# Chunked attention and a multiplicative feed-forward: other transfer costs and first loads in the planner, zero matmuls in early gaps, a last tile in smaller parts

## The chip, the core and the metric

The kernel runs on one core of a Trainium2 chip. The metric is device time in microseconds (us) of one execution; several executions give a median. A profile of a separate execution gives the span from the first to the last instruction and what each engine did. The engines are TensorE (PE in the views, its weight loads PEld), VectorE (DVE), ScalarE (ACT), GpSimd (POOL) and SyncE (SP). Transfers run on the core's 16 DMA engines. GpSimd issues the loads that cast from f32 to bf16, SP issues the outputs and the transposing transfers.

## The reference

```python
# q, k, v: (8 batches, 8 heads, 576 positions, 64), float32; chunks of 64 positions
scores = scale * np.matmul(q_c, k_c.transpose(0, 1, 2, 4, 3))
scores = scores - np.max(scores, axis=-1, keepdims=True)
attn = np.exp(scores)
attn = attn / (np.sum(attn, axis=-1, keepdims=True) + 1e-09)
out = np.matmul(attn, v_c)
...
x = np.ascontiguousarray(attn_out.transpose(0, 2, 1, 3)).reshape(B * S, H * D)
...
a = x @ w1          # x: 4608 x 512, w1 and w2: 512 x 1024
b = x @ w2
h = a * b @ w3      # w3: 1024 x 1024
return (h @ w_out).astype(np.float32)   # w_out: 1024 x 512
```

## The kernel before

The 4608 tokens are cut into 36 groups of 128 (two chunks of 64 positions of all eight heads). Nine tiles of four groups each (512 tokens) go through the feed-forward. The kernel uses that (a*b) @ w3 @ w_out is (a*b) @ (w3 @ w_out), and first makes the 1024 x 512 product w3o.

A group passes these steps (function `add_group`). Loads of q and k into the tile `raw` (L261, from GpSimd). They are transposed, either by eight TensorE matmuls with the identity (L311, with copies to kT and qd), or, from group 12 on, by a transposing transfer from SP (L315, kqT<-raw, called turning here), with two copies to qd. Scores are eight matmuls of 64 columns (L339, p_sc). VectorE takes the maximum (L347) and subtracts it (L351), ScalarE takes the exponential (L355), VectorE sums (L359) and scales (L365, result `an`). `an` is transposed by four TensorE matmuls and a copy (L370), or, from group 24 on, by a transfer from SP (L321, at<-an). Values are eight matmuls of 64 columns (L381, p_av), and a copy writes the group's columns of xt. The buffers for `raw` are six, so the load of q and k for a group waits for an earlier group's transposition.

The product w3o takes eight steps (`add_w3o`): eight transposes of one block of w3 (L422), a copy, eight matmuls of 512 columns (L433, in two parts, one for each load of w_out), a copy. It runs in between the first groups.

A tile (`add_tile`) makes for each of eight column blocks j the products with w1 and w2 (L463, four matmuls of 512 columns each), a copy of the one (ScalarE) and the multiplication (VectorE, L472, abT). For each of its four groups follow eight matmuls with w3o (L488), a copy to o_sb and an output from SP (L497). The last group of the last tile has its 512 output columns in two halves.

The order of everything is set by a planner in the kernel (`Plan.run`) that plays the work through with costs given in microseconds: for each engine it picks, of the operations that are ready at that moment, the one with the lowest key (its due time), then the instructions are written in the order so found. Each engine then works strictly in that order, so an operation that waits longer on the chip than in the plan holds up all behind it on its engine. Loads keep the order of the list LOADS, and then go by groups with the v of a batch ahead of its first use. The planner shares the transfer engines between the queue of GpSimd and that of SP, lets each have eight transfers under way, and takes a transfer as usable a `lag` after its end. `LATE` shifts the keys of a group.

Of the kernel before, what the change touches and what calls it, by code (L numbers as in the profile page):

```python
# [14 lines left out]

LOADS = [('qk', 2), ('w3', 3, 4), ('qk', 0), ('qk', 3), ('ident',), ('qk', 1), ('w3', 5, 6), ('w3', 2, 3),
         ('wo', 0, 4), ('wo', 4, 8), ('w3', 0, 1), ('w3', 6, 7), ('v', 0), ('qk', 4), ('w3', 7, 8), ('qk', 5), ('w12', 0,
         2), ('w12', 6, 8), ('w12', 4, 6), ('qk', 6), ('qk', 7), ('w3', 1, 2), ('w12', 2, 4), ('w3', 4, 5), ('qk', 8),  # L20
         ('v', 1), ('qk', 9), ('qk', 10)]
TILES = [4] * 9

TURN_QK = [g >= 12 for g in range(36)]
TURN_A = [g >= 24 for g in range(36)]
LATE = 5


class Op:
# [124 lines left out]
def kernel(  # L154
# [48 lines left out]
    def ps(tag, shape, dt=f32):  # L203
        return psum.tile(shape, dt, tag=tag, name=tag, bufs=BUFS[tag])
# [39 lines left out]
    def load(cost, issue, emit, **kw):  # L244
        return plan.add("POOL", cost, 0, emit, lag=landing, issue=issue, **kw)
# [6 lines left out]
    def load_qk(g):  # L252
        (b0, c0), (b1, c1) = chunks(g)
        parts = [(slice(0, P), b0, c0, 2)] if b0 == b1 else [(halves[0], b0, c0, 1), (halves[1], b1, c1, 1)]
        box = raws[g] = {"ops": []}
        for w, src in enumerate((q, k)):
            for r, b, c, n in parts:
                def emit(eng, w=w, src=src, r=r, b=b, c=c, n=n):
                    if "t" not in box:
                        box["t"] = sb("raw", [P, 2, H, D])  # L260
                    nc.gpsimd.dma_start(box["t"][r, w], src[b, :, c * C:(c + n) * C, :].rearrange("h p d -> p h d"))  # L261
                box["ops"].append(load(0.43 * n, 0.5 + 0.2 * n, emit, takes=() if box["ops"] else ("raw",)))

    def load_v(b):
        v_got[b] = []
        for t in range(2):
            def emit(eng, t=t):
                nc.gpsimd.dma_start(vds[b % len(vds)][halves[t], :, :, t * D:(t + 1) * D].rearrange("p m c d -> p (m c) d"),  # L268
                                    v[b, NM * t:NM * (t + 1)].rearrange("h (c p) d -> p (h c) d", p=C))
            v_got[b].append(load(2.0, 1.17, emit, takes=() if t else ("vd",), after=(zero_v[b % len(vds)],)))  # L270

    def load_w12(j0, j1):
        for dst, w in ((w1_sb, moe_w1), (w2_sb, moe_w2)):
            for t in range(2):
                def emit(eng, dst=dst, w=w, t=t):
                    nc.gpsimd.dma_start(
                        dst[halves[t], :, j0 * P:j1 * P],
                        w[t * NM * D:(t + 1) * NM * D, j0 * P:j1 * P].rearrange("(m d) n -> d m n", d=D))
                o = load(0.33 * (j1 - j0), 0.62, emit)
        for j in range(j0, j1):  # L280
            w12_got[j] = o

    def load_w3(k0, k1):
        def emit(eng):
            nc.gpsimd.dma_start(w3_sb[:, k0:k1, :], moe_w3.rearrange("(ko p) n -> p ko n", p=P)[:, k0:k1, :])
        o = load(1.3 * (k1 - k0), 0.75, emit)
        for i in range(k0, k1):
            w3_got[i] = o

    def load_wo(k0, k1):  # L290
        def emit(eng):
            nc.gpsimd.dma_start(wo_sb[:, k0:k1, :], moe_w_out.rearrange("(ko p) n -> p ko n", p=P)[:, k0:k1, :])
        wo_got.append(load(0.64 * (k1 - k0), 0.75, emit))
        wo_cut.append((k0, k1))


# [2 lines left out]
    def add_group(g, kt, ks, ka, kv):  # L299
# [1 line left out]
        bc = chunks(g)  # L301
        qd = qds[g % len(qds)]

        turned = TURN_QK[g]

        def t_emit(eng):
            t = box["tr"] = ps("ffn", [P, 2, NM, P], bf)
# [78 lines left out]

        got = raws[g]["ops"]
        if turned:
            tr = kc = plan.add("SP", 1.75, kt, qk_turn, after=got, takes=("kqT",), uses=[(got[0], "raw")], lag=2.5, issue=1.3)
            held, cost = [(tr, "kqT")], (0.35, 0.6)  # L390
        else:
            tr = plan.add("PE", 0.46, kt, t_emit, after=got + [made_ident], takes=("ffn",), uses=[(got[0], "raw")], lag=0.2)
            held, cost = [(tr, "ffn")], (0.43, 0.66)
            kc = plan.add(("DVE", "ACT"), cost, kt, k_copy, after=(tr,), takes=("kT",), uses=held)
# [6 lines left out]
        ex = plan.add("ACT", 0.71, ks, exp_emit, after=[sd] + one_e, takes=("e",), uses=[(sd, "sd")])  # L401
        sm = plan.add("DVE", 0.95, ks, sum_emit, after=(ex,), lag=0.05)
        an = plan.add("DVE", 0.7, ks, norm_emit, after=(sm,), takes=("an",), uses=[(ex, "e")])
        if TURN_A[g]:
            ac = plan.add("SP", 0.88, ka, at_turn, after=(an,), takes=("at",), uses=[(an, "an")], lag=2.5, issue=1.3)
        else:
            at = plan.add("PE", 0.23, ka, at_emit, after=(an,), takes=("ffn",), uses=[(an, "an")], lag=0.2)
            ac = plan.add(("DVE", "ACT"), (0.43, 0.66), ka, at_copy, after=(at,), takes=("at",), uses=[(at, "ffn")])
# [42 lines left out]
    def add_tile(g0, n, kab, ko_):  # L451
        box = {}
        w = n * P
        x = xt[:, :, g0 * P:g0 * P + w]
        muls = []
        for j in range(FO):
            def mm(name, wt, j=j):
                def emit(eng):
                    if j == 0 and name == "a":
                        box["abT"] = sb("abT", [P, FO, TT])  # L460
                    t = box[name, j] = ps("ffn", [P, TT])
                    for ki in range(KO):
                        nc.tensor.matmul(t[:, :w], wt[:, ki, j * P:(j + 1) * P], x[:, ki, :],  # L463
                                         start=(ki == 0), stop=(ki == KO - 1))
                return emit

            def a_copy(eng, j=j):
                box["as", j] = sb("a_sb", [P, TT], f32)
                copy(eng, box["as", j][:, :w], box["a", j][:, :w])

            def mul(eng, j=j):
                nc.vector.tensor_mul(box["abT"][:, j, :w], box["as", j][:, :w], box["b", j][:, :w])  # L472

            dep = [w12_got[j]] + [x_done[g0 + i] for i in range(n)] + ([first] if j else [])
            a = plan.add("PE", 0.216 * n, kab(j), mm("a", w1_sb), after=dep, lag=0.2,
                         takes=("ffn", "abT") if j == 0 else ("ffn",))
            first = a if j == 0 else first
            b = plan.add("PE", 0.216 * n, kab(j) + 0.1, mm("b", w2_sb), after=dep, lag=0.2, takes=("ffn",))
            c = plan.add("ACT", 0.18 + 0.11 * n, kab(j) - 1, a_copy, after=(a,), takes=("a_sb",), uses=[(a, "ffn")])
            muls.append(plan.add("DVE", 0.18 + 0.13 * n, kab(j) - 1, mul, after=(b, c), uses=[(b, "ffn"), (c, "a_sb")]))  # L480
        last = g0 + n == NG
        cols = [(tk, 0, D_MODEL) for tk in range(n - last)]
        cols += [(n - 1, x, x + D_MODEL // 2) for x in (0, D_MODEL // 2)] if last else []
        for tk, x0, x1 in cols:
            def o_mm(eng, tk=tk, x0=x0, x1=x1):
                t = box["o", tk, x0] = ps("ffn", [P, D_MODEL])
                for ki in range(FO):
                    nc.tensor.matmul(t[:, :x1 - x0], box["abT"][:, ki, tk * P:(tk + 1) * P], w3o_sb[:, ki, x0:x1],  # L488
                                     start=(ki == 0), stop=(ki == FO - 1))

            def o_copy(eng, tk=tk, x0=x0, x1=x1):
                box["os", tk, x0] = sb("o_sb", [P, D_MODEL], f32)
                copy(eng, box["os", tk, x0][:, :x1 - x0], box["o", tk, x0][:, :x1 - x0])

            def o_out(eng, tk=tk, x0=x0, x1=x1):
                r0 = (g0 + tk) * P
                nc.sync.dma_start(out[r0:r0 + P, x0:x1], box["os", tk, x0][:, :x1 - x0])  # L497

            f = (x1 - x0) / D_MODEL
            key = ko_(tk) + 0.1 * (x0 > 0)  # L500
            o = plan.add("PE", 1.73 * f, key, o_mm, after=muls + w3o_done, takes=("ffn",), uses=[(first, "abT")], lag=0.2)
            c = plan.add(("ACT", "DVE"), (0.16 + 0.45 * f, 0.17 + 0.53 * f), key - 1, o_copy, after=(o,),
                         takes=("o_sb",), uses=[(o, "ffn")])
            outs.append((c, o_out))


# [59 lines left out]
```

## Time and profile before

| | us |
|---|---|
| median of 3 runs | 261.84 (258.81 to 266.3) |
| the profiled execution's own time | 264.01 |
| its span, first to last instruction | 262.2 |
| TensorE busy in it | 238.1 |
| VectorE busy | 175.0 |
| ScalarE busy | 145.9 |
| GpSimd busy (it issues loads) | 102.1 |

The span leaves out what lies around the first and the last instruction, 1.8 us of the profiled execution. In the rows of the views stand a start or a total in us, a length, the engine, the line of the kernel, and result<-operands by the program's names; x is a count. A wait names the engine and line that waited and what ended the wait. The row of slices cuts the span into 40 equal parts and gives the busy share of each in tenths. Matmuls overlap in the pipeline, so TensorE's price for one is read from the distance between starts, as the chain of waits has it, and not from its own duration.

### The profile page before, as it was taken

How to read it: one execution, taken by the hardware profiler on the slowest of the kernel's cores; microseconds unless marked ns; L12 is line 12 of the kernel's file. 1: busy time of each engine (PE TensorE's matmuls, PEld its weight loads, DVE VectorE, ACT ScalarE, POOL GpSimd, SP SyncE). 2: the span in 40 equal slices, each digit the busy share in tenths (PEclk: the TensorE clock that was granted, in tenths of full speed). 3: DMA queues.
4: the chain of work that ended last, by engine and by line, in shares of the span. 5: the costliest groups of instructions: out<-in, count | busy, mean ns of one | idle time of the engine just before them, and what ended most of it. 6: DMA issues, size and time to landing. Idle time of an engine off the chain costs nothing.

```text
span 262.2 us, 4687 instructions
## 1 busy us (share of the span) xinstructions
PE 238.1 (91%) x1736; PEld 125.8 (48%) x1768; DVE 175.0 (67%) x319; ACT 145.9 (56%) x248; POOL 102.1 (39%) x128
## 2 busy tenths in 40 slices
PE   0479999987999999999899999997979999999994
PEld 0354665545555555555445544453434544444442
DVE  5076888776989976997398977995958762223310
ACT  8262664765866684687367367564456554343332
POOL 8964689767785165228344712460000000000000
PEclk9999999999999999999999999999999999999998
DMA  6999999999999999999999999999996521112123
GB/s 54 163 201 172 169 183 168 175 147 114 156 186 136 153 199 135 176 180 187 149 198 157 166 121 182 197 132 153 194 152 160 103 80 42 41 40 80 42 79 121
DMA packets 155910, 37.01 MB, mean 141 GB/s; under 512 B 145008, under 2 KB 150384, under 8 KB 155888
## 3 DMA queue, kind: packets, MB, share of 16 engines
q0 software_dynamic: 118688, 19.41, 105.4%
q1 hardware_dynamic: 37200, 17.31, 38.0%
q8 instruction: 14, 0.23, 0.4%
q14 instruction: 8, 0.07, 0.1%
HBM read 38.80 MB, written 9.44 MB: 184 GB/s over the span
## 4 chain that ended last, share of the span: by engine, by line
PE 65%; DMA 17%; DVE 8%; issue 3%; ACT 2%; POOL 2%; ACTq 0%; DVEq 0%; POOLq 0%
PE ffn L463 34%; PE ffn L488 18%; DMA at<-an 7%; PE ffn L433 5%; DMA vd<-in_v_dram 4%; DMA kqT<-raw 3%; PE p_av L381 3%; DMA raw<-in_k_dram 3%; PE p_sc L339 2%; PE ffn L370 2%; DVE abT L472 2%; PE ffn L311 2%; DVE nm L347 1%; POOL raw L261 1%; DVE sd L351 1%
## 5 line engine op out<-in xcount | busy, mean ns | idle before, releaser
L463 PE MATMUL ffn<-xt,w_sb 128*128 128x512 bf16 x556 | 133.1, 379 | 2.0 <-DVE abT L472 1.1
L463 PEld LDWEIGHTS <-w_sb 128*128 128x128 bf16 x576 | 53.9, 98 | 59.8 <-issue 1.4
L472 DVE TENSOR_TENSOR abT<-a_sb,ffn 128x512 bf16<-128x512 f32 x72 | 49.0, 681 | 42.1 <-PE ffn L463 35.8
L488 PE MATMUL ffn<-w3o_sb,abT 128*128 128x512 bf16 (+1 forms) x287 | 66.4, 373 | 0.5
L223 ACT COPY a_sb<-ffn 128x512 f32<-128x512 f32 x72 | 41.9, 583 | 27.3 <-PE ffn L463 27.0
L261 POOL DMA_DIRECT2D raw<-in_q_dram x40 | 34.2, 857 | 37.9 <-DMA vd<-in_v_dram 14.4
L261 POOL DMA_DIRECT2D raw<-in_k_dram x40 | 34.1, 854 | 31.0 <-DMA vd<-in_v_dram 21.8
L488 PEld LDWEIGHTS <-abT 128*128 128x128 bf16 x296 | 28.0, 98 | 29.5
L223 ACT COPY o_sb<-ffn 128x512 f32<-128x512 f32 (+1 forms) x28 | 15.9, 569 | 27.4 <-PE ffn L488 27.3
L223 ACT COPY qd<-kqT 64x512 bf16<-64x512 bf16 x30 | 18.5, 616 | 19.4 <-DMA kqT<-raw 19.1
L347 DVE TENSOR_REDUCE nm<-p_sc 128x8 f32<-128x512 f32 x36 | 24.3, 674 | 7.2 <-PE p_sc L339 7.2
L355 ACT ACTIVATE e<-sd 128x512 bf16<-128x512 f32 x36 | 22.8, 634 | 8.3 <-DVE sd L351 7.6
L359 DVE TENSOR_REDUCE ss<-e 128x8 f32<-128x520 bf16 x36 | 24.8, 688 | 1.9 <-ACT e L355 1.2
L351 DVE TENSOR_TENSOR sd<-p_sc,nm 128x512 f32<-128x512 f32 x36 | 24.6, 684 | 0.7
L365 DVE TENSOR_TENSOR an<-e,rs 128x512 bf16<-128x512 bf16 x36 | 24.7, 685 | 0.4
L223 ACT CAST xt<-p_av 128x512 bf16<-128x512 f32 x28 | 16.4, 586 | 12.1 <-PE p_av L381 12.0
L381 PEld LDWEIGHTS <-vd 128*128 128x128 bf16 x288 | 13.0, 98 | 14.3 <-issue 4.6
L268 POOL DMA_DIRECT2D vd<-in_v_dram x16 | 18.5, 1162 | 2.9 <-ACT qd L223 1.4
L381 PE MATMUL p_av<-at,vd 128*128 128x64 bf16 x288 | 14.4, 193 | 5.6 <-DMA at<-an 3.3
L433 PE MATMUL ffn<-wo_sb,w3t 128*128 128x512 bf16 x61 | 17.5, 422 | 0.6 <-DVE w3t L225 0.3
L311 PE MATMUL ffn<-ident,raw 128*128 128x128 bf16 x96 | 9.0, 249 | 9.6 <-DMA raw<-in_k_dram 9.6
L339 PEld LDWEIGHTS <-qd 128*128 128x128 bf16 x288 | 12.6, 100 | 7.1 <-DVE qd L225 0.9
(37 smaller groups left out, 149.4 us busy)
## 6 DMA issues: line engine op xcount, KB each, us to landing
out_dram<-o_sb SPq DMA_DIRECT2D x35, 256.0 KB, 6.4
vd<-in_v_dram POOLq DMA_DIRECT2D x16, 288.0 KB, 15.6
raw<-in_q_dram POOLq DMA_DIRECT2D x32, 128.0 KB, 10.2
raw<-in_k_dram POOLq DMA_DIRECT2D x32, 128.0 KB, 9.6
w_sb<-in_moe_w_dram POOLq DMA_DIRECT2D x8, 256.0 KB, 7.0
w_sb<-in_moe_w_dram POOLq DMA_DIRECT2D x16, 128.0 KB, 5.2
wo_sb<-in_moe_w_out_dram POOLq DMA_DIRECT2D x2, 512.0 KB, 9.7
raw<-in_q_dram POOLq DMA_DIRECT2D x8, 64.0 KB, 16.1
```

Of the source, the lines that this page charges most:

```text
L223: nc.scalar.copy(o, i)
L261: nc.gpsimd.dma_start(box["t"][r, w], src[b, :, c * C:(c + n) * C, :].rearrange("h p d -> p h d"))
L347: nc.vector.tensor_reduce(nm[:, :, 0], flat(box["sc"]), axis=AX.X, op=ALU.max)
L351: nc.vector.tensor_sub(sd[:], flat(box["sc"]), box["nm"].to_broadcast([P, 8, C]))
L355: nc.scalar.activation(e[:, :, :C], box["sd"][:], ACT.Exp, scale=scale)
L359: nc.vector.reduce_sum(ss[:], box["e"][:], axis=AX.X)
L365: nc.vector.tensor_mul(an[:], box["e"][:, :, :C], box["rs"].to_broadcast([P, 8, C]))
L381: nc.tensor.matmul(t[:, m, cc, :], vds[b % len(vds)][:, m, c, :], box["at"][:, 2 * cc + y, u * C:(u + 1) * C], start=True, stop=True)
L433: nc.tensor.matmul(box["wp"][:], box["t"][:, ki, :], wo_sb[:, ki, :], start=(ki == 0), stop=(ki == FO - 1))
L463: nc.tensor.matmul(t[:, :w], wt[:, ki, j * P:(j + 1) * P], x[:, ki, :], start=(ki == 0), stop=(ki == KO - 1))
L472: nc.vector.tensor_mul(box["abT"][:, j, :w], box["as", j][:, :w], box["b", j][:, :w])
L488: nc.tensor.matmul(t[:, :x1 - x0], box["abT"][:, ki, tk * P:(tk + 1) * P], w3o_sb[:, ki, x0:x1], start=(ki == 0), stop=(ki == FO - 1))
```

## The change

Only the kernel's Python that plans and writes the instructions is changed; what is computed stays the same.

- The list LOADS has another order of the first loads: the same pieces, but the first half of w_out third, other pairs and blocks of w3 first, and the last quarter of w1 and w2 just ahead of the second v. Group 10's q and k now stand ahead of group 9's.
- Planned costs of loads rise: q and k 0.43 to 0.45 for each chunk, v 2.0 to 2.05 for each half, w1 and w2 0.33 to 0.41, w3 1.3 to 1.45, w_out 0.64 to 0.72. The lag of SP's transposing transfers rises from 2.5 to 3.5.
- `an` is turned by transfer from group 22 on, not 24. The shift of keys for these groups is 2, not 3; the key of a turned group's q and k is 31 units ahead, not 30.
- One bf16 tile of zeros (128 x 512) is set by VectorE ahead of all else. TensorE multiplies zeros into the bank of p_av: 14 matmuls ahead of its first planned operation, and in each later planned gap as many as fit at 0.25 us each, until the first operation on values. As built there are 47 such matmuls, 33 of them after the first operation.
- The last group's output has parts of 256, 128 and 128 columns. The eight matmuls for the last tile's first group are planned as six and two, so that the first six need only six of the eight products abT.

```diff
-LOADS = [('qk', 2), ('w3', 3, 4), ('qk', 0), ('qk', 3), ('ident',), ('qk', 1), ('w3', 5, 6), ('w3', 2, 3),
-         ('wo', 0, 4), ('wo', 4, 8), ('w3', 0, 1), ('w3', 6, 7), ('v', 0), ('qk', 4), ('w3', 7, 8), ('qk', 5), ('w12', 0,
-         2), ('w12', 6, 8), ('w12', 4, 6), ('qk', 6), ('qk', 7), ('w3', 1, 2), ('w12', 2, 4), ('w3', 4, 5), ('qk', 8),
-         ('v', 1), ('qk', 9), ('qk', 10)]
+LOADS = [('qk', 0), ('wo', 0, 4), ('qk', 3), ('ident',), ('w3', 0, 1), ('qk', 1), ('qk', 2), ('w3', 2, 3),
+         ('qk', 4), ('w3', 4, 5), ('wo', 4, 8), ('v', 0), ('w3', 5, 6), ('w3', 3, 4), ('w12', 0, 2), ('w12', 4, 6),
+         ('qk', 5), ('w12', 2, 4), ('qk', 6), ('w3', 6, 7), ('w3', 7, 8), ('qk', 7), ('w3', 1, 2), ('qk', 8), ('w12', 6,
+         8), ('v', 1), ('qk', 10), ('qk', 9)]
...
-TURN_QK = [g >= 12 for g in range(36)]
-TURN_A = [g >= 24 for g in range(36)]
-LATE = 5
+TURN_QK, TURN_A = 12, 22
+LATE, LATE_A = 5, 2
+AHEAD = [31, 28, 25, 19, 16]
...
-                box["ops"].append(load(0.43 * n, 0.5 + 0.2 * n, emit, takes=() if box["ops"] else ("raw",)))
+                box["ops"].append(load(0.45 * n, 0.5 + 0.2 * n, emit, takes=() if box["ops"] else ("raw",)))
...
-            v_got[b].append(load(2.0, 1.17, emit, takes=() if t else ("vd",), after=(zero_v[b % len(vds)],)))
+            v_got[b].append(load(2.05, 1.17, emit, takes=() if t else ("vd",), after=(zero_v[b % len(vds)],)))
...
-                o = load(0.33 * (j1 - j0), 0.62, emit)
+                o = load(0.41 * (j1 - j0), 0.62, emit)
...
-        o = load(1.3 * (k1 - k0), 0.75, emit)
+        o = load(1.45 * (k1 - k0), 0.75, emit)
...
-        wo_got.append(load(0.64 * (k1 - k0), 0.75, emit))
+        wo_got.append(load(0.72 * (k1 - k0), 0.75, emit))
...
-            tr = kc = plan.add("SP", 1.75, kt, qk_turn, after=got, takes=("kqT",), uses=[(got[0], "raw")], lag=2.5, issue=1.3)
+            tr = kc = plan.add("SP", 1.75, kt, qk_turn, after=got, takes=("kqT",), uses=[(got[0], "raw")], lag=3.5, issue=1.3)
...
-        if TURN_A[g]:
-            ac = plan.add("SP", 0.88, ka, at_turn, after=(an,), takes=("at",), uses=[(an, "an")], lag=2.5, issue=1.3)
+        if g >= TURN_A:
+            ac = plan.add("SP", 0.88, ka, at_turn, after=(an,), takes=("at",), uses=[(an, "an")], lag=3.5, issue=1.3)
...
-        cols += [(n - 1, x, x + D_MODEL // 2) for x in (0, D_MODEL // 2)] if last else []
+        cols += [(n - 1, x0, x1) for x0, x1 in ((0, 256), (256, 384), (384, D_MODEL))] if last else []
...
+            cuts = (0, FO - 2, FO) if last and not tk else (0, FO)
...
-            o = plan.add("PE", 1.73 * f, key, o_mm, after=muls + w3o_done, takes=("ffn",), uses=[(first, "abT")], lag=0.2)
+            mms = []
+            for i in range(len(cuts) - 1):
+                mms.append(plan.add("PE", 0.216 * f * (cuts[i + 1] - cuts[i]), key, o_mm(i), after=muls[:cuts[i + 1]] + w3o_done + mms,
+                                    takes=() if i else ("ffn",), uses=[(first, "abT")], lag=0.2))
...
-        late = min(LATE if not TURN_A[g] else 3, g // 2)
-        add_group(g, *(3 * g - n + late for n in (30 if TURN_QK[g] else 28, 25, 19, 16)))
+        late = min(LATE if g < TURN_A else LATE_A, g // 2)
+        add_group(g, *(3 * g - n + late for n in AHEAD[:1] * (g >= TURN_QK) + AHEAD[1 + (g >= TURN_QK):]))
...
     with tc.manual_schedule():
+        zeros = consts.tile([P, TT], bf)
+        nc.vector.memset(zeros[:], 0.0)
+        warm = ps("p_av", [P, TT])
+        fills, last, cold = 14, 0.0, True
         for o in plan.run():
+            if o.engine == "PE":
+                cold = cold and "p_av" not in o.takes
+                if last:
+                    fills = int((o.start - last - 0.2) / 0.25)
+                for _ in range(fills if cold else 0):
+                    nc.tensor.matmul(warm[:], zeros[:, :P], zeros[:], start=True, stop=True)
+                last = o.start + o.cost
             o.emit(o.engine)
```

More of the change, by code (lines that the diff above doesn't have):

```diff
@@ L302, in add_group @@
         qd = qds[g % len(qds)]
-        turned = TURN_QK[g]
+        turned = g >= TURN_QK
         def t_emit(eng):
@@ L482, in add_tile, with o_mm, emit @@
         cols = [(tk, 0, D_MODEL) for tk in range(n - last)]
-        cols += [(n - 1, x, x + D_MODEL // 2) for x in (0, D_MODEL // 2)] if last else []
+        cols += [(n - 1, x0, x1) for x0, x1 in ((0, 256), (256, 384), (384, D_MODEL))] if last else []
         for tk, x0, x1 in cols:
[L485 to L489, printed above, removed]
+            cuts = (0, FO - 2, FO) if last and not tk else (0, FO)
+            def o_mm(i, tk=tk, x0=x0, x1=x1, cuts=cuts):
+                def emit(eng):
+                    if not i:
+                        box["o", tk, x0] = ps("ffn", [P, D_MODEL])
+                    t = box["o", tk, x0]
+                    for ki in range(cuts[i], cuts[i + 1]):
+                        nc.tensor.matmul(t[:, :x1 - x0], box["abT"][:, ki, tk * P:(tk + 1) * P], w3o_sb[:, ki, x0:x1],
+                                         start=(ki == 0), stop=(ki == FO - 1))
+                return emit
             def o_copy(eng, tk=tk, x0=x0, x1=x1):
@@ L499, in add_tile @@
             f = (x1 - x0) / D_MODEL
-            key = ko_(tk) + 0.1 * (x0 > 0)
-            o = plan.add("PE", 1.73 * f, key, o_mm, after=muls + w3o_done, takes=("ffn",), uses=[(first, "abT")], lag=0.2)
-            c = plan.add(("ACT", "DVE"), (0.16 + 0.45 * f, 0.17 + 0.53 * f), key - 1, o_copy, after=(o,),
-                         takes=("o_sb",), uses=[(o, "ffn")])
+            key = ko_(tk) + 0.1 * x0 / D_MODEL
+            mms = []
+            for i in range(len(cuts) - 1):
+                mms.append(plan.add("PE", 0.216 * f * (cuts[i + 1] - cuts[i]), key, o_mm(i), after=muls[:cuts[i + 1]] + w3o_done + mms,
+                                    takes=() if i else ("ffn",), uses=[(first, "abT")], lag=0.2))
+            c = plan.add(("ACT", "DVE"), (0.16 + 0.45 * f, 0.17 + 0.53 * f), key - 1, o_copy, after=mms,
+                         takes=("o_sb",), uses=[(mms[0], "ffn")])
             outs.append((c, o_out))
```

## Prediction

> **What bounds the kernel now.** I read the page's head and its row of slices first, then who waited for whom on TensorE, then the chain of work that ended last in order of time, then the timeline at the places where TensorE stands.
>
> ```profile
> span 262.2 us, 4687 instructions
> ...
> PE 238.1 (91%) x1736; PEld 125.8 (48%) x1768; DVE 175.0 (67%) x319; ACT 145.9 (56%) x248; POOL 102.1 (39%) x128
> ...
> PE   0479999987999999999899999997979999999994
> ...
> PEclk9999999999999999999999999999999999999998
> DMA  6999999999999999999999999999996521112123
> ```
>
> TensorE is busy nearly everywhere except the first three slices, and the transfers are busy until slice 30 (about 196 us). So two resources run side by side: TensorE, and the transfer engines, which decide when its operands arrive. The waits that TensorE itself shows (reason: us in total, times, longest):
>
> ```profile
> PE ffn L311 <- DMA raw<-in_k_dram: 9.6, 3, 7.9
> PE p_av L381 <- DMA at<-an: 3.3, 2, 1.9
> PE p_av L381 <- DMA vd<-in_v_dram: 2.2, 1, 2.2
> PE ffn L463 <- DVE abT L472: 1.1, 1, 1.1
> ```
>
> Beyond the start, TensorE loses 6.6 us in four waits. From the chain (start, length, what):
>
> ```profile
> 12.97 1.03 PE ffn L311 x8
> ...
> 20.88 1.06 PE ffn L433 x2
> ...
> 22.36 4.09 PE ffn L433 x12
> ...
> 26.91 0.45 PE ffn L422 x8
> ...
> 38.31 3.51 PE ffn L463 x16
> ...
> 49.20 11.15 DMA vd<-in_v_dram
> 60.49 0.28 PE p_av L381 x4
> ...
> 65.17 0.23 PE p_sc L339 x8
> ...
> 67.13 0.23 PE p_av L381 x8
> ...
> 70.23 1.73 PE ffn L463 x8
> ...
> 121.64 8.75 DMA kqT<-raw
> ...
> 172.82 9.93 DMA at<-an
> 182.89 0.39 PE p_av L381 x8
> ...
> 184.77 9.25 DMA at<-an
> 194.06 0.41 PE p_av L381 x8
> ...
> 258.83 0.37 ACT o_sb L223
> ```
>
> The same eight transposes take 1.03 at 13 us and 0.45 at 27 us, and a 512-column matmul 0.53 at 21 us, 0.34 in the mean at 22 to 26 and 0.216 (1.73/8) at 70 us. So TensorE works at half speed in the first 25 us, although the row of granted clock already shows 9 there. Warm prices per block: 0.46 for eight transposes (0.23 for four), 0.23 for eight score or value matmuls, 0.216 for one of 512 columns. The whole program before is 928 of 512 columns' worth (576 L463, 288 L488, 64 L433) = 200.4, 36 score and 36 value blocks 16.6, 96+64+96 transposes 14.7: 231.7 us. TensorE ends at 258.8, so 27.1 us are lag: time that has passed less work done.
>
> I follow this lag through both orders. "Work ahead" of a block is the same sum over what stands before it in the built order of TensorE. Before: first L463 at 38.3 with 19.1 ahead, lag 19.2; the second half of group 4's values at 60.49 with 39.1 ahead, lag 21.4; group 22's scores at 132.73 (row below) with 110.1 ahead, 22.6; group 27's values at 182.89 with 157.7, 25.2; group 29's at 194.06 with 167.2, 26.9; then no wait to the end, 27.1.
>
> **The change part by part.**
>
> *Zeros.* 47 matmuls of 512 columns: 14 ahead of the first transposes, 33 in gaps that the plan foresees before the first value block; one memset ahead of all of VectorE's work.
>
> ```profile
> 0.81 0.06 DVE L231 MEMSET nought<- 128x1 f32 x1 [0.81 <-PEq L550]
> 0.95 0.48 DVE L227 MEMSET qd<- 128x512 uint32 x1
> ...
> 7.90 1.03 PE L311 MATMUL ffn<-ident,raw 128*128 128x128 bf16 x8 [7.90 <-DMA raw<-in_k_dram]
> ...
> 29.21 4.38 POOL L276 DMA_DIRECT2D w_sb<-in_moe_w_dram  x7 [0.59 <-DMA vd<-in_v_dram]
> ```
>
> The memset has half the words of the 0.48 us one, about 0.25. The 14 zeros at half speed take 14 x 0.43 = 6.0 us, from 1.1 to 7.1: before 7.9, when the first k lands, so they are hidden. The 33 cost 33 x 0.216 = 7.1 us. Their cover is the first v: GpSimd, held by it, goes on at 29.2, so v lands at 28.9. In the new order two w3 blocks fewer and one q,k pair more stand ahead of it, about the same sum. Ahead of the first value block stand 9.0 us of work: 7.9 + 9.0 + 7.1 = 24.0, 5 us to spare. So zeros cost nothing (7.1 if v came at once, which the row excludes), and full speed gains nothing by itself either: the lag at that block cannot be under 28.9 - 9.0 = 19.9.
>
> *First loads.* Both orders put the same transfers (nine q,k pairs, the first v, all weights) ahead of the second v, which lands at 60.35 (49.20 + 11.15). I leave it there. The changed order has 14.7 ahead of the first L463 against 19.1, and 39.6 ahead of the waiting half block against 39.1. TensorE reaches it at 39.6 + 19.9 to 20.9 (19.9 is the bound above; the two w3 blocks behind v, each with a transfer and a copy of its own to wait for, I put at up to 1), 59.5 to 60.5. Taken: 60.5, because v itself comes at 60.35; lag 20.9, 0.5 below before. Best: 59.5; worst: the nearest row of a late load is the wait of 2.2 us, so 62.7.
>
> *Transfer costs, keys, lag of 3.5.* No instruction, only order: scores of groups 13 to 21 stand 1.7 to 2.8 us later, values of groups 26 and 28 to 30 by 3.2 to 6.5. What is late next is group 22:
>
> ```profile
> 130.42 0.28 DVE L225 COPY qd<-kqT 64x512 bf16<-64x512 bf16 x1 [4.52 <-DMA kqT<-raw]
> ...
> 132.73 0.39 PE L339 MATMUL p_sc<-kqT,qd 128*128 128x64 bf16 x8
> ...
> 139.86 0.68 DVE L365 TENSOR_TENSOR an<-e,rs 128x512 bf16<-128x512 bf16 x1
> ...
> 170.80 1.26 SPq L315 DMA_TRANSPOSE kqT<-raw  x1
> 172.16 0.58 SPq L497 DMA_DIRECT2D out_dram<-o_sb  x1
> 172.82 1.29 SPq L321 DMA_TRANSPOSE at<-an  x1
> ```
>
> Its turned q,k land at 130.4 and the copies took 1.2 beyond. The transfers were full, so this stays: scores at 131.6, while TensorE with 109.6 ahead would be there at 130.5. A wait of 1.1, lag 22.0. (If the loads come as much earlier as TensorE: none.)
>
> *Groups 22, 23 turned by transfer.* Gone: two times 0.23 of transposes and two copies beside other work. New: two transfers on SP's queue.
>
> ```profile
> at<-an SPq DMA_TRANSPOSE x9, 8.1
> ...
> at<-an SPq DMA_TRANSPOSE x4, 2.4
> ```
>
> (Median from issue to landing, issued from 130 to 200 us and after 200.) Group 22's probabilities are ready 7.8 after its scores (140.5 - 132.7), at 139.4; landed at 147.5. Its values have 124.4 ahead and are due at 146.4: a wait of 1.1, lag 23.1. Range 0 (landing as after 200 us) to 2.9 (9.93 as the longest row). Behind that transfer on SP wait an output and group 26's q,k, whose load lands later anyway. Group 23: scores at 114.6 + 22.0 = 136.6, landed 7.8 + 8.1 later at 152.5; values due at 131.2 + 23.1 = 154.3: none.
>
> *The two late waits.* Before, SP stood at group 31's q,k until 170.8 with group 27's transfer queued behind; in the new order 27's goes first, so it lands some 5 us earlier, at 178, and its values are due at 158.1 + 23.1 = 181.2: no wait. Group 29's landed at 194.0; due at 173.7 + 23.1 = 196.8: no wait. Both (3.3 us) go. The narrowest next: group 31, 177.2 ahead, due at 200.3, its transfer behind group 30's; I put 0.5 for it and other small ones. Lag at the end 23.6.
>
> [...]
>
> *Last tile.* Its last output of 512 columns goes in 256+128+128 in place of 256+256, and the first one's eight matmuls may start after six products: the same columns, one copy and one output more.
>
> ```profile
> L223 ACT COPY o_sb<-ffn 128x512 f32<-128x512 f32 x4 | 2.3, 585 | 6.3 <-PE ffn L488 6.3
> L223 ACT COPY o_sb<-ffn 128x256 f32<-128x256 f32 x2 | 0.7, 372 | 0.8 <-PE ffn L488 0.8
> ```
>
> A copy falls from 0.37 towards 0.27 (half of the 0.21 between the two rows), the transfer a little: 0.2 gained; bounds 0 and 0.4 (one more output issue).
>
> **Sum.** Work: 231.7 - 0.46. Against before: lag 27.1 to 23.6 is 3.5, work 0.46, tail 0.2: 4.2. Span 262.2 - 4.2 = 258.0. The profiled execution took 264.01, so 259.8; it is 0.8% above the shown median of 261.84, whose runs go from 258.81 to 266.3. On the median's scale: 257.6.
>
> **The rivals.**
>
> A. Full speed from the start carries through. By 25 us before, seven blocks of eight transposes (3.2), three of scores (0.7), four transposes (0.2) and ten L433 (2.2) are done at half speed: 6.3 us dearer than warm. If loads come as early as TensorE could use them, that and all four waits go: 6.3 + 6.6 + 0.7 = 13.6, 248 on the median's scale; halfway to the forecast, 253. For it: the rows of 1.03 against 0.46. Against it: the transfers, 9 in every slice, and the wait for the second v, which would only grow.
> [...]
>
> B. The planned waits only move. If `at` lands late for groups 22, 23 and 28 to 31 as it did twice before (1.9 at the longest), the 3.3 won is paid again: 261 (257.6 + 3.3). For it: 14.8 us of work between group 22's scores and values, against 7.8 + 8.1. Against it: values 28 to 30 stand 5 to 6 us later.
>
> C. Slower: zeros do not raise the clock. Before, 17 us of interrupted work did not, and only the dense stretch from 20 to 25 did. Then the first value block comes at 7.9 + 2 x 9.0 + 33 x 0.43 = 40.1 in place of 28.9, lag 31.1; the waits of group 22 vanish behind it, and the work after is at full speed: end lag 31.6, 4.5 over before, less 0.7: 261.84 + 3.8 = 265.6; with cold work for longer, 270. It decides once the cold stretch outlasts the 5 us of cover, about 20 us. Against it: 14 zeros back to back are 6 us, longer than that stretch.
>
> **Chances.** Forecast, 255 to 260: 0.50. A: 0.18. B, no real change: 0.20. C: 0.12. Two per cent is 5.2 us (256.6 and 267.1), about what a measurement of this kernel can tell from no change. Faster by more: A's 0.17 and half of the forecast's lower half and its best bounds, 0.23: 0.40. Slower by more: 0.08 from C. Within: 0.52. The forecast's own range is 254.5 to 260; with B and part of A and C, 252 to 265 for 8 in 10.
>
> **What would show it.** Zeros: the first L311 still near 7.9 and eight transposes at 0.46 to 0.6 from then on (C: 1.03). Loads: the second v landing near 60 and no wait over 0.5 for it (A: well before 58). Group 22: a wait of 1 to 1.5 before its scores, and one near 1 before its values. Late: no wait for `at` at groups 27 and 29 (B: 3 us in total). Tail: 3.2 from the last matmul to the end. Wrong would be above all that the loads land at the times of before: if the new first order moves the second v by 3 us either way, everything behind it moves along.

## The result and the profile after

| us | before | after |
|---|---|---|
| median, 18 runs each on one chip | 262.65 (258.81 to 267.88) | 258.48 (256.34 to 259.82) |
| the profiled execution's own time | 264.01 | 258.48 |
| its span | 262.2 | 256.7 |
| TensorE's last matmul ends, the last copy starts | 258.83 | 253.44 |

The ratio after to before is 0.9896 [0.9859, 0.9932]. It leaves out runs of a kernel that lie over 1.5% above its fastest, which takes more from before, whose runs spread wider, so the medians differ by more (4.17 us, 1.6%). Forecast were 4.2 us; the chance of "within 2%" (0.52) came in. The profiled execution of before was a long one (1.4 over this median), that of after is its median: of the 5.5 us between the spans, some 1.4 are that.

From the page of the changed kernel: the head, TensorE's row, and the rows of slices.

```profile
span 256.7 us, 4818 instructions
...
PE 246.9 (96%) x1815; PEld 127.6 (50%) x1815; DVE 177.0 (69%) x327; ACT 141.9 (55%) x240; POOL 102.2 (40%) x128
...
PE   8889599999999999999999999999999999999994
...
PEclk9999799999999999999999999999999999999999
DMA  7999999999999999999999999999999341111114
```

TensorE is now busy from the first slice, and the three slices with 7 near 62, 180 and 193 us are gone. New is a 5 in the fifth slice (26 to 32 us) with a 7 in the granted clock. The waits of TensorE over the whole span (engine, result, line, what ended it: us in total, times, longest):

```profile
PE p_av L381 <- DMA vd<-in_v_dram: 2.0, 1, 2.0
PE p_sc L339 <- DVE qd L225: 1.4, 2, 0.7
PE p_av L553 <- DVE nought L231: 1.2, 1, 1.2
PE ffn L311 <- DMA raw<-in_k_dram: 0.8, 2, 0.4
PE p_av L381 <- DVE xt L225: 0.8, 1, 0.8
PE p_sc L339 <- DVE sd L351: 0.2, 1, 0.2
```

All of them lie before 30 us. Of the 6.6 us of four waits behind the start that before showed, nothing is left. The timeline of TensorE at the start, and where group 22's scores and values come:

```profile
1.19 5.30 PE L553 MATMUL p_av<-zeros 128*128 128x512 bf16 x14 [1.19 <-DVE nought L231]
6.89 0.62 PE L311 MATMUL ffn<-ident,raw 128*128 128x128 bf16 x8 [0.40 <-DMA raw<-in_k_dram]
...
25.88 0.75 PE L370 MATMUL ffn<-ident,an 128*128 128x128 bf16 x8
28.67 0.39 PE L381 MATMUL p_av<-at,vd 128*128 128x64 bf16 x8 [2.04 <-DMA vd<-in_v_dram]
29.85 0.61 PE L381 MATMUL p_av<-at,vd 128*128 128x64 bf16 x8 [0.78 <-DVE xt L225]
30.27 1.04 PE L422 MATMUL ffn<-ident,w_sb 128*128 128x128 bf16 x8
...
131.48 0.40 PE L339 MATMUL p_sc<-kqT,qd 128*128 128x64 bf16 x8
...
146.28 0.40 PE L381 MATMUL p_av<-at,vd 128*128 128x64 bf16 x8
```

The zeros run before the first k is there. Behind them eight transposes take 0.46 (6.89 to 7.35, the start of what follows) where before they took 1.03: full speed from 5.5 us on. Then TensorE stands 2.04 us for the first v, and at 30.27 the same eight transposes are back at 1.04. The view of windows (stretch, length, busy us and count of PE, PEld, DVE, ACT, POOL, granted clock, DMA share, GB/s) shows why:

```profile
22.56:25.97 3.41, 3.24 (x31) 1.57 (x30) 3.31 (x7) 1.40 (x3) 0.61 (x1) 1.00 2.74 155
25.97:29.38 3.41, 1.06 (x19) 0.65 (x15) 2.44 (x6) 3.34 (x6) 1.17 (x2) 1.00 1.33 199
29.38:32.80 3.42, 2.95 (x23) 2.14 (x24) 2.51 (x5) 1.45 (x2) 2.38 (x5) 0.50 1.43 191
32.80:36.20 3.40, 3.40 (x40) 2.21 (x39) 2.58 (x4) 1.17 (x3) 3.40 (x6) 1.00 1.79 152
```

The clock is granted at full from 5.49 to 29.38, at half from 29.38 to 32.80, then at full to the end of the work. The 23.89 us at full are seven times 3.413, and the fall lasts 3.41: the changes here come in steps of that length. One stretch in which TensorE was busy for 1.06 of 3.41 us is followed by one at half.

### The profile page after: what moved, and what is told of

Its sections match the earlier page's. It is cut to its first block, busy times and chain, and to the rows that moved or that the text cites. A ratio compares the mean times of both kernels' runs of the same rounds, so it can differ in the third digit from the quotient of the medians.

```text
span 256.7 us, 4818 instructions
## 1 busy us (share of the span) xinstructions
PE 246.9 (96%) x1815; PEld 127.6 (50%) x1815; DVE 177.0 (69%) x327; ACT 141.9 (55%) x240; POOL 102.2 (40%) x128
## 4 chain that ended last, share of the span: by engine, by line
PE 87%; DMA 7%; POOL 3%; issue 1%; DVE 0%; ACT 0%; POOLq 0%
PE ffn L463 48%; PE ffn L493 24%; PE ffn L433 4%; DMA vd<-in_v_dram 4%; PE p_av L381 3%; PE p_sc L339 3%; DMA raw<-in_k_dram 3%; PE ffn L370 2%; POOL raw L261 2%; PE ffn L311 1%; PE ffn L422 1%; POOL wo_sb L292 1%; POOL vd L268 0%; POOL w_sb L285 0%; DVE xt L225 0%
## 5 line engine op out<-in xcount | busy, mean ns | idle before, releaser
L463 PE MATMUL ffn<-xt,w_sb 128*128 128x512 bf16 x576 | 134.7, 379 | 0.0
L493 PE MATMUL ffn<-w3o_sb,abT 128*128 128x512 bf16 (+2 forms) x304 | 67.6, 368 | 0.0
L223 ACT COPY o_sb<-ffn 128x512 f32<-128x512 f32 (+2 forms) x32 | 17.9, 558 | 37.6 <-PE ffn L493 35.4
L359 DVE TENSOR_REDUCE ss<-e 128x8 f32<-128x520 bf16 x36 | 24.8, 688 | 6.9 <-ACT e L355 6.7
L223 ACT COPY qd<-kqT 64x512 bf16<-64x512 bf16 x29 | 17.8, 615 | 2.1 <-DMA kqT<-raw 1.9
L223 ACT CAST xt<-p_av 128x512 bf16<-128x512 f32 x24 | 14.1, 586 | 6.8 <-PE p_av L381 6.7
L433 PE MATMUL ffn<-wo_sb,w3t 128*128 128x512 bf16 x64 | 16.7, 390 | 0.0
L553 PE MATMUL p_av<-zeros 128*128 128x512 bf16 x47 | 13.6, 433 | 1.2 <-DVE nought L231 1.2
```

Source lines behind the costliest of these rows:

```text
L223: nc.scalar.copy(o, i)
L359: nc.vector.reduce_sum(ss[:], box["e"][:], axis=AX.X)
L433: nc.tensor.matmul(box["wp"][:], box["t"][:, ki, :], wo_sb[:, ki, :], start=(ki == 0), stop=(ki == FO - 1))
```

## The experiments

Two theories stood against each other. P: the gain is the planned order; the loads' costs and the lag of 3.5 put TensorE's work where its operands are already there, and the waits behind 45 us go. Z: the gain is full speed from the start, by the zeros. A third question came up with the clock that falls: what is a wait at 28 us worth, and who takes it back. The table has the median of each kernel and of before on the same chip, the ratio, and from each profile TensorE's waits behind 45 us and the lag of its last matmul's start (231.7 of work for e11 and for the kernels that turn `an` from group 24 on, 231.3 for the others). Before has 6.6 and 26.8 there, after 0 and 21.9. e1 to e4 and e9 have 6 runs each, e10 has 10, the others 12.

| kernel | median | before | ratio | waits | lag |
|---|---|---|---|---|---|
| e1 changed, no zeros | 259.57 | 262.35 | 0.9967 [0.9896, 1.0038] | 0.2 | 20.1 |
| e2 before + zeros | 262.85 | 262.35 | 1.0129 [1.0072, 1.0187] | 5.1 | 25.1 |
| e3 before + costs + lag | 258.74 | 262.35 | 0.9973 [0.9914, 1.0033] | 2.5 | 21.9 |
| e4 changed, lag 2.5 | 259.08 | 262.35 | 0.9968 [0.9909, 1.0027] | 1.3 | 23.0 |
| e5 changed, again | 258.72 | 261.94 | 0.9915 [0.9873, 0.9956] | 1.6 | 22.0 |
| e6 changed, zeros at first v too | 257.80 | 261.94 | 0.9874 [0.9833, 0.9914] | 2.1 | 24.9 |
| e7 changed, old LOADS | 258.15 | 261.94 | 0.9905 [0.986, 0.9951] | 1.4 | 20.4 |
| e8 before + costs | 260.36 | 261.94 | 0.9932 [0.9879, 0.9986] | 4.1 | 24.8 |
| e9 e6 with lag 4.5 | 257.85 | 261.47 | 0.9872 [0.9829, 0.9916] | 0.4 | 21.1 |
| e10 e7 with lag 4.5 | 259.51 | 261.47 | 0.9954 [0.991, 0.9997] | 2.0 | 21.6 |
| e11 e6, q and k turned from 13 on | 258.21 | 261.47 | 0.9906 [0.9867, 0.9945] | 0.3 | 20.5 |
| e12 changed, old turns | 259.88 | 261.47 | 0.9928 [0.989, 0.9967] | 0 | 22.7 |

A profile is one execution; that of e6 is the longest of its 12 runs (261.52), that of e1 the shortest of 6 and that of e7 the second shortest of 12. So the medians and ratios judge, and the profiles say where. The medians and the ratios don't always order the kernels alike; where they differ, the text gives both.

### What carries the gain: e1 to e4, e8

e1 takes the zeros away:

```diff
-        zeros = consts.tile([P, TT], bf)
...
-                for _ in range(fills if cold else 0):
-                    nc.tensor.matmul(warm[:], zeros[:, :P], zeros[:], start=True, stop=True)
```

> The changed kernel without the memset and the 47 zero matmuls; all else, and the order of all else, as in it. Theory P (planned order: the gain comes from waits after 60 us that are gone, and the start only has to hold): the first value block still waits for the first v at 28.5 us, because 9.0 us of work at half speed, 18 us, still fits between 6.8 and 28.5; only the dense stretch behind it, some 3.5 to 5 us at half speed until the clock rises, costs, 1.7 to 2.5 us, and no wait after 60 us returns: ratio to before 0.996 to 1.000 (changed kernel 0.9896). Theory Z (full clock early is the gain): all of it goes, 1.000 to 1.010, TensorE behind by 4 us or more at 60 us.

Measured: by the medians 2.8 us of 4.2 remain, in few runs that scatter (256.71 to 261.03); the ratio, 0.9967, lies in P's range. TensorE came to full speed by itself near 16.9 us (eight transposes take 1.04 at 14.24 and 0.61 at 17.09), its profile has no wait worth the name behind 45, and the lag, 20.1, is under that of the changed kernel. What the zeros are worth stays open: 1.1 us by the medians (259.57 against 258.48, on two chips), 0.7% or some 1.9 us by the ratios, and the intervals overlap.

e2 puts the same block of zeros into the kernel before:

```diff
+                for _ in range(fills if cold else 0):
+                    nc.tensor.matmul(warm[:], zeros[:, :P], zeros[:], start=True, stop=True)
```

> The kernel before with the memset and zero matmuls alone (29 of them as its plan has the gaps). Theory P: full speed by 8 us, TensorE reaches group 4's values some 2 to 3 us earlier than the 58 of before and waits that much longer for the second v; the waits after it stay, so ratio 0.993 to 1.000. Theory Z: 0.980 to 0.990.

Measured: no gain (0.5 us more by medians, 1.3% by the ratio, which is over P's range too). From its waits behind 45 us:

```profile
PE p_av L381 <- DMA at<-an: 1.7, 2, 1.1
PE p_sc L339 <- ACT qd L223: 1.0, 1, 1.0
PE p_av L381 <- DMA vd<-in_v_dram: 0.8, 1, 0.8
PE ffn L422 <- DMA w_sb<-in_moe_w_dram: 0.6, 1, 0.6
PE ffn L311 <- DMA raw<-in_k_dram: 0.6, 1, 0.6
```

TensorE is earlier at the first values (28.7 us, before 31.1), but not at group 4's (58.7, before 58.0), where P had expected it 2 to 3 us earlier; then it waits for four kinds of transfers and for a copy. Z falls: an earlier start isn't what the old order lacks. The clock, though, was not at full all the time: the mean of the profiled execution is 0.992, where one stretch of 3.41 at half makes it 0.993 (the changed kernel's).

e3 gives the kernel before only the planner's numbers, and e8 only those of the loads (the first line of each kind below, shortened):

```diff
-load(0.43 * n, ...   load(2.0, ...   load(0.33 * ...   load(1.3 * ...   load(0.64 * ...
+load(0.45 * n, ...   load(2.05, ...   load(0.41 * ...   load(1.45 * ...   load(0.72 * ...
-            tr = kc = plan.add("SP", 1.75, ... lag=2.5, issue=1.3)
+            tr = kc = plan.add("SP", 1.75, ... lag=3.5, issue=1.3)
-            ac = plan.add("SP", 0.88, ... lag=2.5, issue=1.3)
+            ac = plan.add("SP", 0.88, ... lag=3.5, issue=1.3)
```

> The kernel before with the new planned costs of loads and the lag of 3.5 alone: old first loads, no zeros, old turns and keys, old last tile. Theory P: the waits for group 22's copies and for the turned probabilities of groups 27 and 29 (4.9 us in the trace of before) are mostly gone, ratio 0.984 to 0.990, nearly the whole gain. Theory Z: 0.997 to 1.003.

Measured for e3: 3.6 us less than before by medians, with the lag of the changed kernel, 21.9. The ratio doesn't bear this out: 0.9973 lies in Z's range and not in P's, and its interval reaches 1.0033. It rests on the five of eleven runs of before that it keeps on this chip, which average 259.84; e3's six average 259.14. So the size rests on the medians and on one profile, whose waits behind 45 us name no transfer any more:

```profile
PE ffn L433 <- ACT w3t L223: 1.1, 1, 1.1
PE p_sc L339 <- DVE sd L351: 1.1, 1, 1.1
PE p_sc L339 <- ACT qd L223: 0.3, 1, 0.3
```

> The kernel before with the new planned costs of loads alone, the lag still 2.5. With costs and lag together it gave 258.74 and one late wait of 1.2 us. If the lag does it: late waits for turned probabilities of 2 us and more in total, time 260.5 to 263. If the costs do it: 258 to 260 and at most one wait over 1 us after 60 us.

Measured for e8: 1.6 us less than before by medians, with 0.6 of waits for `at` left and 1.9 for copies of ScalarE. The median lies just outside the ranges of both cases, and the waits fit neither. By the medians the loads' costs carry somewhat under half of e3's 3.6 us and the lag the rest; by the ratios e8 (0.9932) is ahead of e3, so this split isn't shown. e4 asks the same from the other side, the changed kernel with the two lags at 2.5 again:

> The changed kernel with the lag of SP's transposing transfers at 2.5 again; start, loads, zeros as in it. Values of group 24 then stand at 136.8 us of work ahead in place of 142.0, those of group 29 at 168.5 in place of 173.7, while group 24's turned probabilities landed at 161.8 us with a lag of 22 due at 158.8. Theory P: waits of 1 to 3 us for turned probabilities come back at groups 24 to 29, ratio 0.995 to 1.003. Theory Z: no change from 0.9896.

```profile
PE p_av L381 <- DMA at<-an: 1.3, 1, 1.3
```

The only wait behind 45 us is the kind that the lag was for: the values of a group whose turned probabilities are on their way, group 22's at 146.5 us and not one of 24 to 29. Lag 23.0, about 1 us over the changed kernel; the ratio, 0.9968, is in P's range, but its interval and that of the changed kernel overlap. P fits e1, e4, the medians and the profiles better than Z does; that the planner's numbers carry most of the gain is likely, and not shown by the ratios.

### The wait for the first v and the clock: e5, e6

e5 is the changed kernel once more, beside e6 on one chip:

> The changed kernel itself once more, beside the next three. In its first trace the granted clock fell to half from 29.4 to 32.8 us, behind the wait for the first v (2.0 us), and the lag at group 4's values was 21.9 where 20.9 was forecast. Theory D (an unfilled wait lets the clock fall for one window of 3.4 us, which costs about 1.7 us): here too a stretch of 3.4 us at half speed stands behind that wait whenever the wait is 2 us or so, and the lag at group 4 is 21.5 to 22.2. Theory L (the lag at the start is the transfers' alone): the lag does not follow the clock.

e6 sets eight zeros ahead of the first block of values, where the loop of the change has stopped:

```diff
-                cold = cold and "p_av" not in o.takes
...
+                if cold and "p_av" in o.takes:
+                    fills = 8
                 for _ in range(fills if cold else 0):
                     nc.tensor.matmul(warm[:], zeros[:, :P], zeros[:], start=True, stop=True)
+                cold = cold and "p_av" not in o.takes
```

> The changed kernel with 8 more zero matmuls (1.7 us) ahead of the first value block, where it stands waiting for the first v. Theory D: the clock stays up, the L433 behind take 0.86 for four and not 1.45, lag at group 4 20.0 to 20.6, and with no wait behind it the whole span is 1.3 to 2 us shorter: median 256.5 to 257.3 beside 258.5. Theory L: no change in lag or time, 258.0 to 259.0.

Measured: 257.80, between the ranges of the two theories and 0.9 us under e5, with intervals that overlap; the lag at group 4 is 20.7. Clearer is the mean granted clock that comes with each run. Of the 30 runs of the changed kernel (18, and 12 of e5), 22 show 0.985 to 0.993, that is one or two stretches at half; of the 30 runs of e6, e9 and e11, which have the eight zeros, 5 do. In the 18 runs, five without a stretch at half average 257.28, eleven with one 258.71, two with two 259.68: 1.4 us for the one and 1.0 for the second, which two runs alone show. Those of e6 without one average 257.69, as the undisturbed ones of e5 (257.72): no gain of the eight zeros shows beyond keeping the clock.

In e5's profile the clock doesn't fall, though TensorE waits almost as long, which theory D had not expected; the lag at group 4, 20.0, follows the clock, which theory L had not:

```profile
28.12 0.39 PE L381 MATMUL p_av<-at,vd 128*128 128x64 bf16 x8 [1.75 <-DMA vd<-in_v_dram]
...
131.31 0.41 PE L339 MATMUL p_sc<-kqT,qd 128*128 128x64 bf16 x8 [1.62 <-ACT qd L223]
```

It rose at 3.88; with the step of the changed kernel's profile a stretch ends 23.89 later, at 27.77, in the middle of the wait. The two stretches have 1.83 and 2.23 us of work:

```profile
24.36:27.77 3.41, 1.83 (x20) 0.88 (x18) 3.34 (x8) 2.95 (x6) 0.61 (x1) 1.00 1.89 188
27.77:31.18 3.41, 2.23 (x35) 1.72 (x37) 2.73 (x6) 2.26 (x4) 1.78 (x3) 1.00 1.38 192
```

So in these two executions where the stretches happened to lie decided whether much the same wait (2.04 and 1.75) cost itself alone or some 1.4 us more. And what e5 wins there it loses at group 22: its turned q,k come at 130.0, and the scores wait 1.6. The profile of e6 shows that wait longer, and inside one stretch. From its chain (start, length, what), its timeline and its windows:

```profile
120.54 10.70 DMA kqT<-raw
```

```profile
132.56 0.41 PE L339 MATMUL p_sc<-kqT,qd 128*128 128x64 bf16 x8 [2.12 <-ACT qd L223]
...
133.28 3.56 PE L493 MATMUL ffn<-w3o_sb,abT 128*128 128x512 bf16 x8
```

```profile
129.83:133.24 3.41, 1.27 (x22) 0.78 (x22) 0.37 (x2) 1.92 (x4) 1.47 (x2) 1.00 2.10 161
133.24:136.65 3.41, 3.41 (x12) 1.22 (x10) 3.34 (x7) 1.49 (x3) 1.03 (x2) 0.50 1.61 156
```

Eight matmuls of 512 columns take 3.39 (133.28 to 136.67) where they take 1.73 at full speed. That is e6's longest run; three of its 12 runs, 260.86 to 261.52, stand apart from the other nine, all three at 0.993, as do two of e11's (261.17 and 261.19). Where those other four fell isn't known.

### Load order, later turning: e7, e9 to e12

e7 is the changed kernel with before's LOADS (34 zeros as built):

> The changed kernel with the first loads in the old order (zeros, 34 by its plan, costs, lag, turns and last tile as in it). If the new order of loads is worth something, the lag at group 4 is higher than 21.9 and the time over 259. Theory P (the waits after 60 us are what counted): no wait after 60 us either way, lag at group 4 20 to 21.5, time 257.5 to 259.

Measured: no worse than e5 beside it (258.15 against 258.72), with a lag of 20.0 at group 4 and one wait behind 45 us of 1.1, near 52. The new order of the first loads is worth nothing that shows here.

e9 asks whether a lag of 4.5 takes away the wait at group 22, e10 the same with before's LOADS:

```diff
-            tr = kc = plan.add("SP", 1.75, ... lag=3.5, issue=1.3)
+            tr = kc = plan.add("SP", 1.75, ... lag=4.5, issue=1.3)
-            ac = plan.add("SP", 0.88, ... lag=3.5, issue=1.3)
+            ac = plan.add("SP", 0.88, ... lag=4.5, issue=1.3)
```

> The changed kernel with 8 zeros ahead of the first value block, and a lag of 4.5 in place of 3.5 for SP's transposing transfers. With a full clock TensorE is at group 4 with a lag of 20.0 to 20.7 and then waited 1.7 to 2.3 us for the copies of group 22, whose turned q,k land at about 130. In this order group 22's scores have 111.8 of work ahead, not 109.6, so they are due at 132 or later. Theory O (what counts is where the order puts the block that a late transfer feeds): no wait at group 22, end lag 20.3 to 21.2, median 256.3 to 257.5. Theory T (the transfers are simply full, and a wait not taken at group 22 comes back at another group): end lag 21.8 to 22.5, median 258 to 259.

> The changed kernel with the old first loads and a lag of 4.5. With 3.5 it had an end lag of 20.5 in its trace and 258.15 in the median. Theory O: the same or slightly better, 256.5 to 258; the first loads make no difference to e9_fill_lag45 beyond 1 us. Theory T: 258 to 259.

Measured: in e9's profile the wait is gone and the end lag is 21.1, as theory O has it, and its six runs have no stretch at half, but the median is that of e6, 0.35 us over O's range. e10 came out 1.5 us over O's range and 0.5 over T's, with 0.9 us of waits for `at`; none of its ten runs has a stretch at half. It is 1.7 us over e9, where at most 1 was expected from the first loads; the intervals overlap a little, so whether the first loads matter at this lag stays open. A lag of 4.5 shows no gain over 3.5.

e11 goes back to TensorE for one group's q and k (`TURN_QK` 13 in place of 12, on e6), to shorten SP's queue:

> The changed kernel with 8 zeros ahead of the first value block, and group 12 turned by TensorE and not by a transfer: one transposing transfer fewer ahead of group 22, eight transposes more (0.46). Its plan puts group 22's scores at 107.5 of work ahead, due at 127.8 to 128.2. If the wait at group 22 is set by the amount of transfers ahead of it: its q,k land 1 to 2 us earlier, at 128 to 129, and the wait is 1 to 2.5 us, as the plan has also moved the scores earlier; no gain, 257.5 to 259. If the order decides (theory O): the same, a wait of 2 to 3.5 us, since the scores stand 2.1 us earlier and q,k land where they did, near 130.

Measured: a wait of 0.3 at group 22 in its profile, whose q,k land at 126.7, earlier than either case expected; but in e7 they land at 126.6 with the old number, and the median isn't under e6's. Not settled, and not a gain that shows.

e12 has before's numbers for turning and keys in the changed kernel:

```diff
-TURN_QK, TURN_A = 12, 22
-LATE, LATE_A = 5, 2
-AHEAD = [31, 28, 25, 19, 16]
+TURN_QK, TURN_A = 12, 24
+LATE, LATE_A = 5, 3
+AHEAD = [30, 28, 25, 19, 16]
```

> The changed kernel with the old turns and keys (probabilities turned by transfer from group 24 on, shift 3, q,k 30 units ahead). Work is 0.46 more. If the new turns matter only by that work: 0.2 to 0.7 us over the changed kernel, 258.8 to 259.4, no wait at turned probabilities. If they matter by the order: waits at groups 24 to 29, 260 or more.

Measured: 1.6 us less than before where the changed kernel had 3.2 to 4.2, with no wait behind 45 us in the profile. That is over the range for the work alone, and without the waits of the other case. 0.46 us is work; another part is the clock, which fell for two stretches here:

```profile
24.75:28.16 3.41, 1.63 (x19) 0.78 (x17) 3.18 (x7) 3.09 (x6) 0.61 (x1) 1.00 1.62 193
28.16:31.57 3.41, 2.47 (x28) 2.29 (x30) 2.58 (x4) 1.42 (x3) 2.25 (x4) 0.50 1.42 193
31.57:34.98 3.41, 3.27 (x21) 2.04 (x21) 1.49 (x3) 1.03 (x2) 3.41 (x6) 0.50 1.74 174
```

Eight of its 12 runs show 0.984 to 0.993. Since nothing ahead of 35 us differs from the changed kernel, this is the same wait for v. What is left for the new turns isn't told apart from nothing. The parts of the last output were not tried alone.

By its interval only e2 is told apart from the changed kernel; e6 and e9 have the lowest ratios.

## Why the prediction came out, step by step

*Zeros: cost nothing, gain nothing by themselves.* That they gain nothing by themselves e2 bears out; what they add in the new order e1 leaves open, and 0.7% would be more than the forecast has. One detail failed. "5 us to spare" ahead of the first value block was counted as cover, and not as a wait: the loop stops there, TensorE stands, and the clock that the zeros raised goes again. From the first values to group 4's the lag grows by 0.8 us at full clock (e5, e6, e9, e11), by 2.2 and 2.5 with one stretch at half (the changed kernel's profile, e4) and by 3.6 with two (e12): 1.4 to 1.7 us for a fall that the forecast didn't have. In the changed kernel's profile a wait of 2.04 us, in a stretch with 1.06 us of work, was enough for it.

*First loads: second v at 60.35, lag 20.9.* The lag was forecast between the two cases that occur (20.0 and 21.9). The landing was off: the second v came at 57.7 in the changed kernel, and at 56.4 to 59.7 in the profiles of the experiments, with the old LOADS too. 60.35 was the late end of a spread, read from one execution. So no wait for it, as forecast, with more room than forecast. That it came 2.7 us early, close to the 3 us named as a sign of being wrong, moved nothing behind it: TensorE reached group 4's values at 61.35.

*Group 22's scores: a wait of 1.1, lag 22.0.* The number came out, 21.8, in the changed kernel's profile, but not by the forecast's mechanism: the turned q,k landed at 127.1 and not at 130.4, the scores didn't wait, and the lag is what the fallen clock had left (21.9 at group 4's values). That is luck. The same program in e5, with the clock up, shows the mechanism: q,k at 130.0, a wait of 1.6, a lag of 21.7. In e6 they come at 131.2 and the wait is 2.1. In e7, e9 and e10 there is no wait and in e11 one of 0.3 (lag 20.1 to 20.5 there), so it isn't a fixed time.

*Group 22's values: a wait of 1.1.* Wrong in size, and the term that was furthest off: the probabilities were ready sooner, so the transfer was issued at 137.9 (6.4 us behind the scores in place of 7.8), it landed at 144.8, 6.9 us later in place of 8.1, and the values at 146.28 didn't wait. In the changed kernel the transfers of `at` issued from 130 to 200 us took a little less than before, those of q and k no less (median us from issue to landing). Before, beside the 8.1 of `at`:

```profile
kqT<-raw SPq DMA_TRANSPOSE x12, 9.4
```

After:

```profile
kqT<-raw SPq DMA_TRANSPOSE x12, 9.8
at<-an SPq DMA_TRANSPOSE x11, 7.5
```

The 8.1 of before came from nine, two of which were the late ones that no wait follows any more. The two new turns put off GpSimd's loads by nothing that shows: the last load lands at 195.5, before at 195.9.

*The two late waits go.* Right. Group 27's turned probabilities went ahead of group 31's q and k on SP:

```profile
165.62 1.25 SPq L321 DMA_TRANSPOSE at<-an  x1
166.96 0.53 SPq L503 DMA_DIRECT2D out_dram<-o_sb  x1
167.58 1.39 SPq L321 DMA_TRANSPOSE at<-an  x1
169.19 3.17 SPq L315 DMA_TRANSPOSE kqT<-raw  x1
```

Group 27's (167.58) landed at 175.4, forecast 178, for values at 179.9; group 29's at 189.8 for values at 195.6. The 0.5 put for small ones was not needed.

*Last tile: 0.2.* The last copy starts 3.37 us from the end of the span before (262.2 - 258.83) and 3.26 after (256.7 - 253.44): 0.1. The chain's end:

```profile
246.45 6.96 PE ffn L493 x48
253.41 0.02 issue
253.44 0.27 ACT o_sb L223
```

*Sum.* The end of the work, 253.44, less 231.3 is a lag of 22.1, forecast 23.6: 1.5 too much, 1.1 for the values of group 22 and 0.5 for the small ones. Against the profile of before that makes 5.0 of lag, 0.46 of work and 0.1 of tail: the 5.5 us between the spans. On the medians the gain was 4.17, forecast 4.2: the 1.4 us that was over-long in the profile of before, and the 1.5 that I put too much at the end, nearly cancel. And at group 22 a fall of the clock stood in for the wait that was forecast. The medians' agreement is better than the working deserves.

*Rivals.* A fell: the time is 258.48 and not 248 to 253, and full speed at the start does not carry through (e2, and e5 at group 22). B fell: no planned wait came back, and where the lag is the old one, 1.3 does (e4). C fell at once, at 5.49 us.

## What to carry to other kernels

Where an order is planned ahead, the planned price of a transfer acts far behind its place: with prices 3 to 24% higher and a lag 1 us longer, the waits at 131, 183 and 194 us were gone in the profile (e3). By the medians these numbers alone gave 3.6 us, most of the gain; the ratio of that run doesn't tell it from nothing. Filler work that is to hold the clock has to reach over the wait that it is for, here the last one before the first values: 22 of 30 runs without the eight zeros there had a stretch or two at half, 5 of 30 with them. A landing time read from one execution is one of a spread: group 22's q and k landed at 127.1 and at 130.0 in two executions of the same program. A gain that hangs on such a time gets both ends.

## What the runs showed of the hardware

- The clock here goes by stretches of 3.41 us (after: 23.89 at full, seven of them, then one at half). In three stretches at full clock that were followed by half clock TensorE was busy for 1.06, 1.27 and 1.63 us (after, from 25.97; e6, from 129.83; e12, from 24.75). In others that were not, it was busy for 1.83 and 2.23 (e5, from 24.36 and 27.77), for 1.96 (before, from 192.53), and, by estimate, for 1.6 in e1, 3.41 less the wait of 1.82 (17.70 to 19.52) in its first stretch at full speed; eight transposes still take 0.61 at 20.64. So no whole stretch of standing idle was needed, and by busy time the line, near half a stretch in these rows, isn't sharp.
- Stretches at half clock with 2.21 to 2.55 us busy (before, 8.21 to 21.86, where the row of the clock shows full and eight transposes take 1.03) and with 2.47 (e12) did not raise it; those with 2.95 (after), 3.27 (e12) and 3.41 (before, e6) did. So a fall lasted one stretch in dense work, and two in e12, where the next one held 2.47.
- Matmuls of zeros raised the clock: in the changed kernel it was at full from 5.49 us on, with zeros from 1.19 on and no other work of TensorE before.
- The clock does not explain the scatter of before: of its 73 runs beside the experiments, the 24 at a mean clock of 1.0 go from 257.94 to 264.58. What does is open, since one execution of it has a profile; the waits for transfers, fewer in the new order, are the likely part and not shown to be it; the changed kernel's 18 runs spread over 3.5 us, those of before beside them over 9.
